# Turning the keys, queries and outputs of three batches on TensorE in place of DMA, under another written order

## The chip, the core and the metric

The kernel runs on one core of a Trainium2 chip. The core has a matrix engine (TensorE, "PE" in the profile, with its weight loads as "PEld"), a vector engine (VectorE, "DVE"), a scalar engine (ScalarE, "ACT"), GpSimd ("POOL") and the sync engine ("SP"), which here only issues transfers. Each works through a queue of its own, in order, and waits on semaphores for the others. The metric is the time of one execution on the device in microseconds (us); lower is better. Times of the kernel before: 255.43 us, the median of 3 runs (255.31 to 255.56).

## What is computed

Eight batches of eight heads, 576 positions, head size 64. First an attention with random features, then a gated long convolution on its output:

```python
def phi(x):                                   # 128 features for each position
    proj = einsum('bhsd,md->bhsm', x, omega)
    h = proj - sum(x * x, -1) / 2
    return exp(h - max(h)) / sqrt(m)
q_p, k_p = phi(q * scale), phi(k * scale)
kv  = einsum('bhsm,bhsd->bhmd', k_p, v);  z = sum(k_p, over s)
x   = (q_p @ kv) / (q_p @ z + 1e-6)           # batch, 576, 512

proj = x @ w_proj                             # 512 -> 3 * 512: x1, x2, x3
x2c  = irfft(rfft(x2, n=576) * rfft(filter, n=576), n=576)   # along the 576 positions
out  = (x1 * x2c * x3) @ w_out
```

## The kernel before

**Stages.** Positions are cut into four tiles of 128 and a rest of 64; the rests of two batches share a tile. `attention()` and then `hyena()` describe the work batch by batch. For a batch `b` the attention part does this. `turn_keys` brings the natural keys (positions on partitions) into the turned form `kt` (head dimension on partitions). `key_features` multiplies `kt` with the turned `omega` on TensorE, 64 rows to a matmul, and ScalarE takes the exponential into `ek`. VectorE finds the maxima of `ek` and scales the values into `vc` (`weigh_values`). `turn_queries` makes `qt`, and TensorE and ScalarE make `eqt`. "Sums" multiplies `ek` with `vc` into `kv`. "Turn out" multiplies `eqt` with `kv`, VectorE divides (`normalise`), and the result, with positions on partitions, is turned into `xt` (channels on partitions). `hyena()` handles two batches at a time: `fold`/`fold_rest` and `project2` for x2, `forward` (a Fourier transform as matmuls with tables, evicted into `sp`, whose two halves of partitions are swapped by two DMAs into a second `sp` tile, then multiplied with the filter's spectrum by VectorE in `spectrum`), `gates` (x1 and x3), "inverse", and "out" (the product with `w_out`, scaled by ScalarE, stored).

**Turning.** There are two ways. On TensorE, `transposes`, `turn_back` and `turn_runs` put eight 128x128 transposes (matmuls with the identity `ident`) into one bank of PSUM, named `h` (four such banks rotate among all users), and one copy brings the bank to SBUF: VectorE's for `kt`, ScalarE's for `qt` (from batch 2) and `xt`. By DMA, `cross` issues one transposing DMA on the SP queue for the whole tile. The table `CROSSED` (line 24) says from which batch on the DMA is taken. Before, it is batch 5 for keys, queries and outputs, so 9 transposing DMAs in all:

```python
crossed = {n: b >= first for n, first in CROSSED.items()}
def cross(dst, src):
    nc.sync.dma_start_transpose(out=dst, in_=src)
```

When outputs are crossed, `normalise` writes into `xb4`, one tile in the buffer `h1` that `max_to_c` uses too (one buffer); otherwise into four small buffers `xb`, which "inverse" shares for its `yc` and `yu`.

**Order.** Nothing runs in the order in which it is described. `Plan.record` (line 180) keeps every instruction as an operation with a number (matmuls into one bank in a row are one operation), and `Plan.issue` (line 232) issues them in the order of the list `ORDER` (line 26), which is written out by hand into the file and fixes the order of each engine's queue, the SP and POOL queues among them. Each number must stand behind those whose data it needs. As everything is issued from two lines, the profile's rows name L248 (a recorded operation) or L237 (below); one tells rows apart by the tiles that they write and read.

**Idle products.** `FILL` (line 91) names operations ahead of which `issue` puts a number of products of `ones` with itself (128x128 by 128 columns) into the bank that the operation is about to write. Their result is overwritten; they keep TensorE working. Before there are 139 of them at 8 places, on line 237, all in the first part of the kernel ("the ramp" below: the time until TensorE is steadily at work).

Of the kernel before, what the change touches and what calls it, by code (L numbers as in the profile page):

```python
# [13 lines left out]
BF16 = mybir.dt.bfloat16  # L14
# [6 lines left out]

P = 128

CROSSED = {"keys": 5, "queries": 5, "out": 5}

ORDER = """
0 38 43 35 28 30 29 32 44 36 31 33 40 37 39 34 1 8 5 41 42 49 50 51 4 45 140 7 22 56 55 3 11 53 21
10 54 52 2 48 139 68 6 46 23 24 62 25 142 63 64 66 26 75 15 47 57 65 82 83 58 60 59 103 61 101 81 76
77 79 584 84 67 89 69 17 102 78 588 80 605 70 71 90 73 72 157 85 138 587 104 586 74 111 113 115 117
158 137 105 91 151 159 210 106 143 107 108 92 93 94 152 161 112 95 96 97 114 12 9 589 160 165 162  # L30
109 116 163 13 118 590 110 99 164 153 209 166 591 595 20 155 154 156 167 119 120 127 128 130 131 129
145 87 183 184 86 227 124 16 132 125 126 221 121 122 98 185 123 228 630 628 631 645 647 641 18 629
599 598 168 100 186 187 135 136 133 230 646 19 134 173 233 234 222 169 175 146 232 620 144 632 170
174 612 176 594 606 171 593 172 597 633 592 229 231 614 621 178 180 224 613 637 636 643 622 181 642
147 149 662 212 148 226 215 182 663 615 623 211 177 179 204 205 634 596 206 624 14 635 247 664 191
192 194 195 193 248 667 207 638 616 196 640 668 208 626 235 688 218 281 236 188 189 245 690 190 197
293 246 639 618 198 199 223 225 287 200 201 294 689 691 237 608 202 259 203 256 625 238 694 258 692
261 288 239 319 712 644 693 609 240 627 666 713 761 320 697 249 250 695 585 283 217 150 677 610 655
665 213 763 679 219 214 284 678 681 669 611 216 704 290 696 657 292 656 658 659 710 296 298 684 251
252 253 363 762 764 141 705 241 295 297 708 711 600 601 243 709 603 260 289 291 262 602 364 661 357  # L40
757 730 731 670 671 254 255 257 358 263 264 648 728 699 276 672 303 242 304 305 277 660 273 274 680
278 275 301 729 759 302 649 346 617 676 675 366 698 673 360 306 619 362 706 707 299 265 726 758 368
220 282 244 266 703 702 727 300 701 267 700 307 760 685 365 359 361 367 674 769 724 771 268 650 351
654 269 682 345 270 356 725 753 321 313 315 271 770 385 386 322 755 323 308 754 272 387 388 772 756
314 309 311 316 733 718 279 280 369 317 318 716 732 683 719 734 370 310 312 735 872 736 371 714 372
285 715 686 717 340 373 341 604 335 336 342 765 687 383 767 384 343 720 381 332 721 344 857 337 858
423 653 374 333 334 867 723 722 607 382 776 778 327 742 743 324 338 286 339 325 326 777 744 745 746
396 865 780 328 375 866 329 651 779 747 652 398 934 766 936 330 349 417 88 376 331 869 868 870 871
389 768 859 352 740 741 861 790 792 426 378 737 860 390 738 881 739 429 481 348 347 748 749 942 944
428 943 885 791 945 886 431 873 793 794 773 787 775 876 751 874 788 875 395 930 932 397 931 887 789  # L50
888 933 796 425 774 427 483 392 394 950 889 935 795 882 377 379 878 782 750 890 952 430 391 449 879
781 783 893 937 432 450 894 393 907 752 399 472 479 400 908 883 433 451 797 877 784 862 880 804 884
806 801 350 803 409 818 820 863 815 903 798 452 802 410 434 435 411 901 436 473 484 864 453 904 902
412 897 353 355 354 424 898 816 817 486 799 785 413 800 819 905 895 488 414 786 822 821 896 437 938
404 415 405 438 823 906 909 910 940 401 416 838 839 824 951 805 402 406 380 478 825 891 892 403 494
495 808 482 444 446 807 439 441 953 407 919 912 911 809 913 422 447 920 496 408 448 923 917 921 497
498 922 499 810 918 924 490 500 954 467 1135 492 468 811 812 1050 501 983 985 899 840 956 469 900
955 957 939 440 442 443 445 947 941 915 946 958 491 948 1137 487 493 914 489 1051 813 916 814 826
949 827 828 925 960 829 969 971 1127 926 457 454 830 928 959 535 927 455 831 961 1129 456 475 418
477 847 848 849 470 853 460 929 471 854 856 1128 461 458 462 1130 474 421 480 966 970 972 973 835  # L60
463 967 968 836 419 1124 997 420 1011 1065 974 1059 464 999 1060 1013 459 465 1052 561 562 1123 1125
1053 984 855 485 1058 1063 541 538 1062 975 1126 543 540 841 980 1136 981 1061 837 987 976 466 986
512 542 982 977 1138 502 988 1064 832 1147 1066 1082 506 989 544 833 1149 1083 1054 1069 514 1055
1067 507 503 962 1080 1081 964 537 516 1078 1079 518 842 990 991 508 1074 1075 1068 1072 978 834 850
1096 1097 992 851 1076 539 963 509 1071 1025 1026 965 510 476 511 504 843 1070 1027 1077 1031 1032
1033 1100 1101 1008 513 517 1143 515 1012 519 1009 1145 520 545 546 993 536 852 1056 1014 521 1084
1016 547 1015 1057 1010 528 548 1017 1094 1073 529 979 530 994 522 523 1095 1085 995 996 998 1148
1000 505 524 531 1001 532 533 1090 1098 1099 1103 551 1091 1028 1029 1092 1102 525 553 549 1150 1002
526 527 1003 1004 1018 1139 1141 550 1086 1087 555 556 1022 1140 558 557 1110 1111 552 1005 1019
1007 563 564 565 1088 1021 1142 1046 1105 1104 554 559 534 1030 1093 1328 1089 560 1330 569 1258  # L70
1047 1048 1049 1106 570 1144 571 1108 1146 579 1020 1006 1114 1115 1320 1321 1243 580 1244 1176 1322
1023 1323 1178 1112 572 1162 1163 1164 1043 1107 573 1131 1113 1044 1024 1045 1133 1109 1329 574
1165 581 575 566 1166 1331 576 567 577 1132 1159 1160 1161 1177 1040 1134 582 1041 583 568 1252 578
1179 1167 1180 1168 1169 1259 1155 1116 1324 1173 1253 1251 1257 1256 1255 1117 1119 1042 1118 1326
1174 1175 1157 1156 1158 1267 1254 1262 1245 1275 1247 1325 1276 1332 1334 1246 1170 1260 1271 1327
1272 1273 1261 1268 1121 1266 1264 1181 1037 1265 1038 1269 1274 844 1281 845 1270 1293 1289 1282
1120 1182 1122 1171 1183 1172 1151 1294 1290 1153 1184 1204 1287 1206 1263 1185 1288 1291 1205 1190
1292 1295 1296 1333 1186 1208 1207 1248 1335 846 1340 1342 1192 1341 1152 1343 1187 1039 1191 1154
1193 1189 1194 1298 1249 1250 1188 1196 1195 1197 1198 1200 1034 1201 1283 1279 1035 1036 1202 1297
1299 1203 1284 1286 1285 1280 1199 1209 1300 1301 1210 1303 1277 1278 1309 1224 1310 1304 1305 1306  # L80
1225 1211 1212 1218 1219 1220 1307 1308 1312 1226 1370 1369 1371 1302 1214 1373 1372 1316 1366 1368
1367 1374 1375 1376 1213 1377 1344 1346 1345 1355 1318 27 1357 1221 1356 1347 1222 1239 1311 1236
1240 1237 1359 1313 1358 1314 1352 1317 1319 1349 1348 1350 1315 1223 1233 1238 1351 1353 1215 1360
1397 1234 1354 1242 1399 1241 1378 1383 1361 1379 1385 1216 1336 1338 1362 1363 1364 1394 1398 1395
1396 1337 1217 1235 1411 1400 1365 1412 1413 1417 1384 1401 1403 1402 1339 1380 1418 1419 1404 1382
1381 1414 1415 1387 1386 1389 1388 1390 1405 1391 1407 1416 1230 1231 1227 1228 1232 1408 1229 1409
1410 1393 1420 1421 1406 1392 1424 1436 1425 1430 1431 1437 1427 1428 1433 1434 1435 1423 1422 1426
1432 1438 1429
"""

FILL = {
    23: (40,), 75: (48,), 77: (13,), 89: (4,), 101: (6,), 103: (6,), 127: (12,), 135: (10,)
}

SIZE = {FP32: 4, UINT16: 2, BF16: 2, FP16: 2, mybir.dt.uint32: 4}
# [156 lines left out]
def kernel(  # L252
# [11 lines left out]
    nc = Plan(tc.nc, tc)  # L264
# [19 lines left out]
    const = ctx.enter_context(tc.tile_pool(name="const", bufs=1))  # L284
# [47 lines left out]
    def load_left(i, which):  # L332
# [3 lines left out]
        for j in range(2):  # L336
            nc.gpsimd.dma_start(
                out=t_[j * SL : (j + 1) * SL, :, :],
                in_=src[2 * i + j, :, SM:S, :].rearrange("h p d -> p h d"),
            )  # L340
        nat_tiles[which + "l", i] = t_

    nc.at("start", 0)
    nc.ones = nc.tile(const, [P, P], BF16, name="ones")
    nc.vector.memset(nc.ones[:], 1.0)
    om_f = nc.tile(hy, [P, D], FP32, name="osb", bufs=3)
    nc.sync.dma_start(out=om_f[:], in_=omega[:, :])
    ident = nc.tile(const, [P, P], BF16, name="ident")
    fi = nc.tile(const, [P, 5], FP32, name="fi")
    fp = nc.tile(const, [P, 1], FP32, name="fp")  # L350
    si = nc.tile(hy, [P, 512], FP32, name="osb", bufs=3)
# [43 lines left out]
    for j in range(2):  # L395
        nc.vector.tensor_scalar_mul(
            out=om2[j * D : (j + 1) * D, :], in0=omt[:D, :MF], scalar1=qk_scale
# [27 lines left out]
    gta = nc.tile(const, [P, CH], BF16, name="gta")  # L425
    gns = nc.tile(const, [P, 2, CH], BF16, name="gns")
    hps = nc.tile(const, [P, 5, DM], BF16, name="hps")
    hqs = nc.tile(const, [P, 5, DM], BF16, name="hqs")
    lo64, hi64 = slice(0, 64), slice(64, 128)

# [969 lines left out]
```

## Time and profile before

| | before |
|---|---|
| median of 3 runs | 255.43 us |
| the profiled execution's own time | 255.41 us |
| its span, first to last instruction | 253.6 us |
| around the span | 1.8 us |
| mean granted TensorE clock | 0.992 |
| PE busy | 236.9 us, 2370 matmuls in the records |
| VectorE busy | 225.7 us |
| ScalarE busy | 200.8 us |
| GpSimd busy | 59.4 us |
| bytes moved by DMA | 38.12 MB, mean 150 GB/s |
| transposing DMAs | 9, on the SP queue |

How to read it: a matmul's row gives the time from its start to the modelled end of its pipeline, so one of 128 columns shows 219 ns though the next may start sooner. The rate of a stream is read from the starts of rows that follow each other in the timeline. Busy time counts overlapping matmuls once. A few per cent of matmul records are missing.

### The profile page before, as it was taken

How to read it: one execution, taken by the hardware profiler on the slowest of the kernel's cores; microseconds unless marked ns; L12 is line 12 of the kernel's file. 1: busy time of each engine (PE TensorE's matmuls, PEld its weight loads, DVE VectorE, ACT ScalarE, POOL GpSimd, SP SyncE). 2: the span in 40 equal slices, each digit the busy share in tenths (PEclk: the TensorE clock that was granted, in tenths of full speed). 3: DMA queues.
4: the chain of work that ended last, by engine and by line, in shares of the span. 5: the costliest groups of instructions: out<-in, count | busy, mean ns of one | idle time of the engine just before them, and what ended most of it. 6: DMA issues, size and time to landing. Idle time of an engine off the chain costs nothing.

```text
span 253.6 us, 6119 instructions
## 1 busy us (share of the span) xinstructions
PE 236.9 (93%) x2370; PEld 142.6 (56%) x2404; DVE 225.7 (89%) x543; ACT 200.8 (79%) x322; POOL 59.4 (23%) x80
## 2 busy tenths in 40 slices
PE   6968988999999999998999998999999999998992
PEld 6946736645665655465645654564556545455641
DVE  6999999999998899997998998999898997986960
ACT  4799498999999998999779586987865664873772
POOL 8397531674106125700920000000000000000000
PEclk9988999999999999999999999999999999999999
DMA  6999999999949996996999491264622705254266
GB/s 78 186 189 191 206 181 201 221 176 197 209 71 172 184 193 118 165 154 138 189 172 155 144 193 49 85 165 108 124 85 76 173 3 161 67 166 127 83 248 210
DMA packets 87573, 38.12 MB, mean 150 GB/s; under 512 B 58427, under 2 KB 81912, under 8 KB 87544
## 3 DMA queue, kind: packets, MB, share of 16 engines
q0 software_dynamic: 59088, 16.85, 64.6%
q1 hardware_dynamic: 28312, 20.68, 33.4%
q8 instruction: 19, 0.31, 0.5%
q10 hardware_dynamic: 144, 0.20, 0.2%
q14 instruction: 10, 0.08, 0.1%
HBM read 33.72 MB, written 9.44 MB: 170 GB/s over the span
## 4 chain that ended last, share of the span: by engine, by line
PE 67%; ACT 11%; DVE 9%; DMA 8%; issue 3%; POOL 0%; SPq 0%; POOLq 0%; ACTq 0%; DVEq 0%
PE h L248 55%; PE a L248 12%; ACT ek L248 4%; DMA kt<-kn 4%; DVE sp L248 2%; DMA sp<-sp 2%; ACT eqt L248 2%; DMA xt<-h 2%; ACT osb L248 1%; ACT x L248 1%; DVE xb L248 1%; DVE yt L248 1%; DVE vc L248 1%; ACT L248 1%; DVE kt L248 0%
## 5 line engine op out<-in xcount | busy, mean ns | idle before, releaser
L248 PE MATMUL h<-xt,wproj 128*128 128x512 bf16 x242 | 62.7, 379 | 1.9 <-DMA xt<-h 0.6
L248 ACT CAST x<-h 128x512 bf16<-128x512 f32 x68 | 39.7, 603 | 16.6 <-PE h L248 9.6
L248 PEld LDWEIGHTS <-wproj 128*128 128x128 bf16 x384 | 30.6, 98 | 26.7 <-issue 2.9
L248 ACT ACTIVATE osb<-h 128x512 f32<-128x512 f32 (+4 forms) x53 | 30.2, 574 | 7.9 <-PE h L248 6.0
L248 ACT ACTIVATE eqt<-a 128x1024 bf16<-128x1024 f32 x32 | 32.7, 1049 | 1.1 <-PE a L248 1.1
L248 ACT ACTIVATE ek<-a 128x1024 bf16<-128x1024 f32 x32 | 32.6, 1048 | 0.4 <-PE a L248 0.2
L248 PE MATMUL h<-wproj,xf 128*128 128x512 bf16 x123 | 31.8, 379 | 0.4 <-issue 0.2
L248 PE MATMUL h<-wout,yt 128*128 128x512 bf16 (+2 forms) x128 | 31.2, 373 | 0.9 <-DVE x L248 0.7
L248 POOL DMA_DIRECT2D qn<-in_q_dram x26 | 23.4, 909 | 17.9 <-PE h L248 6.9
L248 DVE TENSOR_TENSOR x<-h,x 128x512 bf16<-128x512 f32 x32 | 21.6, 679 | 2.6 <-PE h L248 1.8
L248 ACT CAST sp<-h 128x512 bf16<-128x512 f32 x32 | 18.6, 614 | 4.3 <-PE h L248 4.2
L248 PEld LDWEIGHTS <-yt 128*128 128x128 bf16 x132 | 12.1, 98 | 13.7 <-issue 1.2
L248 PEld LDWEIGHTS <-xf 128*128 128x128 bf16 x128 | 11.6, 98 | 12.3 <-issue 0.9
L248 PEld LDWEIGHTS <-sp 128*128 128x128 bf16 x160 | 13.9, 98 | 5.5 <-DVE xf L248 0.2
L248 POOL DMA_DIRECT2D vn<-in_v_dram x8 | 7.2, 895 | 39.5 <-DVE vc L248 25.9
L248 DVE TENSOR_TENSOR xb<-a,rden 128x512 bf16<-128x512 f32 x24 | 16.0, 677 | 0.2
L248 PE MATMUL h<-x,fwb 128*128 128x512 bf16 x51 | 14.9, 379 | 0.1
L248 PE MATMUL a<-om,kt 64*128 64x128 bf16 x256 | 12.3, 223 | 2.0 <-DMA kt<-kn 0.7
L248 PEld LDWEIGHTS <-eqt 128*128 128x128 bf16 x256 | 11.3, 98 | 4.5 <-DVE xb L248 0.9
L248 PE MATMUL a<-kv,eqt 128*128 128x65 bf16 x256 | 12.8, 194 | 0.5 <-ACT ekl L248 0.2
L248 PEld LDWEIGHTS <-kt 64*128 64x128 bf16 x256 | 7.8, 96 | 9.4 <-issue 6.1
L248 PE MATMUL h<-gtab,sp 128*128 128x192 bf16 x64 | 12.8, 246 | 0.1
(156 smaller groups left out, 512.4 us busy)
## 6 DMA issues: line engine op xcount, KB each, us to landing
out_dram<-osb SPq DMA_DIRECT2D x24, 256.0 KB, 2.8
vn<-in_v_dram POOLq DMA_DIRECT2D x8, 512.0 KB, 8.4
sp<-sp SPq DMA_DIRECT2D x16, 256.0 KB, 3.5
kn<-in_k_dram POOLq DMA_DIRECT2D x7, 512.0 KB, 10.5
qn<-in_q_dram POOLq DMA_DIRECT2D x24, 128.0 KB, 7.9
wproj<-in_moe_w_proj_dram POOLq DMA_DIRECT2D x3, 512.0 KB, 11.6
qn<-in_q_dram POOLq DMA_DIRECT2D x2, 512.0 KB, 8.1
out_dram<-xf SPq DMA_DIRECT2D x4, 256.0 KB, 2.0
```

Of the source, the lines that this page charges most:

```text
L248: getattr(real, name)(*args, **kw)
```

## The change

`CROSSED` becomes 8 for all three, and there is no batch 8. So `cross` is never called, and the branches that batches 0 to 4 take are taken by 5 to 7 too. For each of these three batches, three transposing DMAs go, and six groups come: two for the keys (eight transposes and a VectorE copy each), two for the queries and two for the outputs (eight transposes and a ScalarE copy each). `normalise` then writes `xb` in place of `xb4`. The list has 1466 operations in place of 1439, is wholly rewritten, and numbers after batch 4 have moved. `FILL` holds 145 idle products at 11 places. `ones` has no tile of its own any more: it lies in the first 128 columns of `hps`, which is written with the filter's spectrum only later.

```diff
-CROSSED = {"keys": 5, "queries": 5, "out": 5}
+CROSSED = {"keys": 8, "queries": 8, "out": 8}
 ORDER = """
-0 38 43 35 28 30 29 32 44 36 31 33 40 37 39 34 1 8 5 41 42 49 50 51 4 45 140 7 22 56 55 3 11 53 21
...
-1432 1438 1429
+25 34 39 32 38 40 35 37 33 36 31 28 29 30 4 42 49 41 43 50 51 6 0 1 3 56 55 21 139 5 22 44 68 45 24
...
+1337 1395 1400 1399 1394 1242 1254 1261 1402 1390 1339 1401 1391 1403 1404 1405 1338 1341 1340 1342
+1375 1367 1255 1243 1244 1369 1438 1439 1377 1262 1256 1441 1442 1435 1436 1443 1440 1437 1376 1410
...
+1462 1459 1453 1465 1456
 """
 FILL = {
-    23: (40,), 75: (48,), 77: (13,), 89: (4,), 101: (6,), 103: (6,), 127: (12,), 135: (10,)
+    22: (25,), 69: (3,), 72: (7,), 75: (17,), 78: (61,), 89: (4,), 91: (8,), 101: (4,), 103:
+    (6,), 127: (6,), 157: (4,)
 }
...
     nc.at("start", 0)
-    nc.ones = nc.tile(const, [P, P], BF16, name="ones")
-    nc.vector.memset(nc.ones[:], 1.0)
...
     hps = nc.tile(const, [P, 5, DM], BF16, name="hps")
+    nc.ones = hps[:, 0, 0:P]
+    nc.vector.memset(nc.ones, 1.0)
```

## The prediction, on record before the result

> **What bounds the kernel now.** I read the page's busy times first, then busy time by stage, because a share over the whole span mixes stages.
>
> ```profile
> PE 236.9 (93%) x2370; PEld 142.6 (56%) x2404; DVE 225.7 (89%) x543; ACT 200.8 (79%) x322; POOL 59.4 (23%) x80
> ```
>
> ```profile
> core 0: us, PE busy (x) PEld busy (x) DVE busy (x) ACT busy (x) POOL busy (x), PEclk, DMA share, GB/s
> 0.00:60.00 60.00, 52.63 (x707) 36.57 (x711) 54.96 (x162) 49.95 (x65) 35.08 (x50) 0.97 1.54 181
> 60.00:160.00 100.00, 97.12 (x1002) 56.85 (x1015) 93.18 (x211) 88.96 (x142) 24.30 (x30) 1.00 1.16 153
> 160.00:222.00 62.00, 61.53 (x498) 34.44 (x505) 57.19 (x126) 43.92 (x82) 0.00 (x0) 1.00 0.43 107
> 222.00:245.00 23.00, 21.68 (x152) 12.91 (x153) 19.84 (x47) 14.79 (x32) 0.00 (x0) 1.00 0.45 147
> 245.00:253.60 8.60, 3.92 (x22) 1.80 (x21) 0.50 (x2) 3.16 (x6) 0.00 (x0) 0.98 0.64 221
> ```
>
> From 60 to 222 us TensorE is idle for 2.88 + 0.47 = 3.4 us of 162. Batches 5 to 7 are turned in this stretch (the transposing DMAs start between 77.3 and 194.3 us), so what the change adds to TensorE is added where it has no room. Only the ramp (7.4 us idle) and the end have room.
>
> The chain of waits names the DMA, and so would suggest that much is to be had:
>
> ```profile
> 105.83 0.36 PE a L248 x9
> 106.20 9.48 DMA kt<-kn
> 115.68 0.05 issue
> 115.72 0.40 PE a L248 x8
> ```
>
> But a step of the chain that runs through a DMA counts the whole flight, though TensorE does other work meanwhile. The timeline of TensorE shows what it lost:
>
> ```profile
> 114.38 0.59 PE L248 MATMUL h<-x,fwn 128*128 128x512 bf16 x2
> 115.72 0.40 PE L248 MATMUL a<-om,kt 64*128 64x128 bf16 x8 [0.75 <-DMA kt<-kn]
> ...
> 151.50 1.04 PE L248 MATMUL h<-wout,yt 128*128 128x512 bf16 x4
> 153.12 1.02 PE L248 MATMUL h<-xt,wproj 128*128 128x512 bf16 x4 [0.58 <-DMA xt<-h]
> ```
>
> **The change part by part.** *Transposes on TensorE.* Three batches, six groups each, eight transposes each: 144. Their nearest row is a group that already stands in a dense stretch:
>
> ```profile
> 146.29 0.59 PE L248 MATMUL h<-wproj,xf 128*128 128x512 bf16 x2
> 146.72 0.39 PE L248 MATMUL h<-ident,ql 128*128 128x128 bf16 x4
> 146.95 0.59 PE L248 MATMUL h<-xt,wproj 128*128 128x512 bf16 x2
> ```
>
> Two matmuls of 512 columns take 0.43 us from start to start, 0.215 each; the four transposes move the next start by 0.23 us, 56 to 57 ns each, with nothing lost going in or out. So 144 x 56 ns = 8.1 us, all of it on the path. Two rules of the Trainium skill speak for more. "TensorE: Matmul & The Clock Gate", section "Back-to-back issue gap", puts a stream of weight load and matmul at N=128 at about 81 ns each, which gives 11.7 us. Here each transpose has its own weight load and yet follows after 56 ns, so I take the row and keep 11.7 us for the range. The same page, "Part 4: PE-mode transpose", says that transposes don't count as activity for the clock gate. If turns let the clock fall to half, as it stands in one stretch of this trace (0.51 from 17.6 to 21.1 us), each would cost about 107 ns, 15.4 us together, and slow the matmuls around them. But 112 products with `ident` (transposes of batches 1 to 4 and of rests) lie between 60 and 160 us at a clock of 1.00. A group is 0.45 us long amid matmuls; I take no loss of clock there.
>
> *The transposing DMAs go.* TensorE gets back what the timeline shows: 115.72 - (114.38 + 2 x 0.215) = 0.9 us, and 153.12 - (151.50 + 4 x 0.215) = 0.8 us: -1.7 us. The bounds are 0 (the copy of the new group, or the next operand, is late at the same place) and -3.4 us (all idle time from 60 to 222 us). The SP queue also loses nine issues of 1.8 to 5.1 us; the stores and swaps behind them go earlier. From 60 to 160 us VectorE waits 0.7 us for a swap and TensorE never does, so I take 0 for it.
>
> *Copies.* Rows of the same operation:
>
> ```profile
> L248 ACT COPY qt<-h 128x1024 bf16<-128x1024 bf16 x6 | 6.2, 1038 | 0.0
> L248 DVE COPY kt<-h 128x1024 bf16<-128x1024 bf16 x10 | 6.8, 682 | 0.4 <-PE h L248 0.3
> ```
>
> Twelve ScalarE copies, eight of them for batches 5 and 6: 12 x 1.04 = 12.5 us. Six VectorE copies: 6 x 0.68 = 4.1 us. The division writes `xb` in place of `xb4` (677 against 688 ns): nothing. These lie beside TensorE's work: from 60 to 160 us ScalarE has 11 us to spare and VectorE 7 us, and the stretch itself grows by most of 8 us. I take 0. If that cover is gone, each of the 18 groups holds one of four `h` banks until its copy ends; TensorE losing 0.25 us at each would be +4.5 us. The wait that each copy adds stands in front of the evictions queued behind it, which is the way in which this would show.
>
> *The ramp.* Batches 5 to 7 are not in it; only the order and the idle products change. VectorE (14.1 of 15 us busy from 10 to 25 us, and again from 25 to 40) and ScalarE (14.2 of 15 from 10 to 25) set its pace. I added single durations in both written queues up to the point where TensorE has been given 16 and 32 us of its own work (56 ns for 128 columns, 216 for 512). VectorE has then been given 39.8 before and 38.0 after, and 59.6 before and 56.9 after; at 64 us, 92.5 and 93.5, and ScalarE 88.2 and 85.1. The two ramps are nearly alike, perhaps 1 us better. The first keys are loaded earlier in the POOL queue, but the first exponential still waits for the sines' residues on VectorE and for ScalarE's table loads. Six more idle products are 0.3 us where TensorE waits anyway: 0. A half-clock stretch of 3.4 us more or less is 1.7 us either way. I take -0.5 us, with -3 and +3 as bounds.
>
> *The end.* Before, TensorE has about 11.6 us of work queued between the last forward block of batch 7 and the first inverse block of batch 7, and still waits 0.55 + 0.66 us there. After, 8.5 us stand there (two inverse blocks of batch 6, seven blocks of four matmuls, two of 16). The data need: cast 0.6 and latency 0.2, second swap issued 0.5 later, 3.5 us (the median of the swaps) to 5.3 us (this one) to land, three products of 1.22 on VectorE: 8.5 to 10.3. So about 1 us idle, as before. Behind it VectorE has about 8.2 us to do before the last output blocks, plus 0.9 until its first input, while TensorE has 8.1: about 0.8 us more. Bounds -0.5 and +2.5.
>
> **Sum**, against the profiled execution's 255.4 us (span 253.6, 1.8 around it, within 0.02 of the median): 255.4 + 8.1 - 1.7 + 0 + 0 - 0.5 + 0.8 = 262.1 us.
>
> **The rivals.** *A, the forecast (0.60):* TensorE is full and takes the transposes at 56 ns: 259.5 to 265, likeliest 262.1.
>
> *B, the turns cost more than their columns (0.18):* copies and banks are the next thing late. Against it: VectorE and ScalarE have room on the average. For it: from 75 to 106 us ScalarE is busy 29.6 of 31 us. With 4.5 us lost at banks: 266.6, between 265 and 269.
>
> *C, the other order wins part of it back (0.12):* the ramp 3 us better and all idle time of the middle gone, 262.1 - 2.5 - 1.7 = 257.9, between 256 and 259.5.
>
> *D, it ends on the other side (0.10, of which 0.02 is no change):* the ramp is the lever. In the first 60 us TensorE is idle for 7.4 us and does 139 idle products (7.8 us): 15.2 us without use. If the new order halves that, 255.4 + 8.1 - 1.7 - 7.6 = 254.2. It decides from 6.4 us won in the ramp. Against it: VectorE is busy for 55 of those 60 us and is given the same work. That the change fails to do what it says can be left out: with 8 in the table no batch reaches `cross`.
>
> **How the numbers follow.** A difference under 0.2% (0.5 us) can't be told from no change here. Predicted 262.1, case A's. The range, 258.0 to 266.5, leaves out D and about half of B. Slower by over 0.2%: A, B and C, 0.90; within 0.2%: 0.02; faster: 0.08.
>
> **What would show it.** Right: no transposing DMA in the list of issues; 144 more products with `ident`, a group of eight moving the next start by 0.45 us; from 60 us on TensorE idle for no more than 3 us until the end; the time from 60 us to the last inverse blocks 6 to 8 us longer; ramp within 1 or 2 us. B shows as idle TensorE or weight loads ended by "ACT qt", "ACT xt" or "DVE kt". C and D show as TensorE reaching the same work of batches 1 and 2 earlier. I am wrong if the middle has room that busy time hides: matmuls count as busy until their modelled end, so small stalls are not seen, and fewer of them in another order would be a gain that no row here foretells.

## The result and the profile after

The kernel after takes 263.92 us (median of 4 runs, 263.01 to 264.29), against 255.38 us (255.31 to 255.56) for the kernel before, run beside it. The ratio is 1.0328 [1.0301, 1.0355]: slower, 1.8 us above the forecast of 262.1 and inside its range. The profiled execution took 264.05 us, with a span of 262.3 us, 8.7 more than before's.

The page's busy times of the kernel after:

```profile
PE 248.5 (95%) x2554; PEld 151.4 (58%) x2554; DVE 230.8 (88%) x549; ACT 212.9 (81%) x334; POOL 59.6 (23%) x80
```

By the pages TensorE is busy 11.6 us longer. Part of that is recording: before lacks the records of 34 of its 2404 matmuls (PE x2370, PEld x2404), after lacks none. Run 12 below has the order of before up to three moves near its end, and all its records. Its page:

```profile
PE 238.4 (94%) x2404; PEld 142.4 (56%) x2404; DVE 225.6 (89%) x543; ACT 200.8 (80%) x322; POOL 59.4 (24%) x80
```

Against this one, after is busy 10.1 us longer. ScalarE has 12.1 us more than before and VectorE 5.1, about the new copies (12.5 and 4.1 us in the forecast). The stages of after, cut as in the prediction:

```profile
core 0: us, PE busy (x) PEld busy (x) DVE busy (x) ACT busy (x) POOL busy (x), PEclk, DMA share, GB/s
0.00:60.00 60.00, 51.59 (x699) 36.78 (x700) 54.10 (x158) 48.54 (x64) 33.70 (x48) 0.97 1.52 173
60.00:160.00 100.00, 98.71 (x1077) 59.63 (x1076) 90.29 (x197) 88.03 (x134) 25.87 (x32) 1.00 0.99 129
160.00:222.00 62.00, 61.91 (x558) 35.60 (x557) 56.10 (x128) 51.97 (x90) 0.00 (x0) 1.00 0.21 64
222.00:245.00 23.00, 23.00 (x137) 12.02 (x135) 20.57 (x46) 15.43 (x31) 0.00 (x0) 1.00 0.44 133
```

From 60 to 222 us TensorE is idle for 1.29 + 0.09 = 1.4 us, and for none of the 23 us behind. The 3.4 us of before, which the prediction took as room, hold gaps where records are missing: run 12, with the same order there, is idle for 1.5 us. So TensorE was about as full before as it is after. The DMAs move less (share 1.16 to 0.99, then 0.43 to 0.21). The products with `ident`, by tile:

```profile
L250 PE MATMUL h<-ident,xb x144: 218/219/230, 31.8 to 211.7; 128*128 128x128 bf16 x144
L250 PE MATMUL h<-ident,kn x128: 217/219/230, 5.8 to 142.2; 128*128 128x128 bf16 x128
L250 PE MATMUL h<-ident,qn x128: 217/219/314, 12.5 to 181.3; 128*128 128x128 bf16 x128
```

Before, these counts are 96, 80 and 80: 48 more each, 144 together. The 219 ns of a row is no price. That is read from the starts of rows, here in TensorE's timeline of after:

```profile
209.09 1.03 PE L250 MATMUL h<-xt,wproj 128*128 128x512 bf16 x4
209.96 0.61 PE L250 MATMUL h<-ident,xb 128*128 128x128 bf16 x8
210.40 1.03 PE L250 MATMUL h<-wproj,xf 128*128 128x512 bf16 x4
211.27 0.61 PE L250 MATMUL h<-ident,xb 128*128 128x128 bf16 x8
211.71 1.03 PE L250 MATMUL h<-wproj,xf 128*128 128x512 bf16 x4
```

A group of eight moves the next start by 0.44 us, as forecast. All 18 new groups do so in this trace, by 0.44 to 0.46 us each and 8.04 us together, which is 56 ns for a transpose. From the matmul ahead of a group to its first transpose less than 0.01 us is lost, but for one group with 0.12. Between 60 and 245 us nothing waits for the new ScalarE copies; one wait of 0.4 us is for a new VectorE copy, of `kt` (waits of TensorE in after, total, times, longest):

```profile
PE h L250 <- DMA sp<-x: 0.7, 2, 0.4
PE h L250 <- DVE kt L250: 0.4, 1, 0.4
PE a L250 <- DVE vcl L250: 0.2, 1, 0.2
```

**Where the 8.7 us lie.** Busy time hides small stalls, so I matched each matmul record with its place in the written order and added columns at the rates of dense stretches: 56 ns for 128 columns, 82.5 for 192, 216 for 512, 30.5 for 65, and half of that for each of two matmuls on different 64 rows. This sum, without idle products, is TensorE's *own work*; what remains between two starts is *loss*. Own work is a count times a rate: its growth says how many columns were added, and only the starts say what they took. The ramp ends when 36 us of own work are done, the end begins when 27 us are left (differences are taken before rounding):

| us | before | after | difference | forecast |
|---|---|---|---|---|
| ramp: time until 36 us of own work are done | 61.8 | 63.4 | +1.6 | -0.5 |
| middle: own work | 150.0 | 158.0 | +8.0 | +8.1 |
| middle: loss | 8.4 | 9.4 | +0.9 | -1.7 (with the copies at 0) |
| end: time for the last 27 us of own work | 33.2 | 31.4 | -1.9 | +0.8 |
| span | 253.6 | 262.3 | +8.7 | |

The large term is right. The three small ones each miss by 2 to 3 us, two upwards and one downwards, and so the sum misses by only 2.

### The profile page after: what moved, and what is told of

The parts are those of the page before. It is cut to its first block, busy times and chain, and to the rows that moved or that the text cites. A ratio compares the mean times of both kernels' runs of the same rounds, so it can differ in the third digit from the quotient of the medians.

```text
span 262.3 us, 6466 instructions
## 1 busy us (share of the span) xinstructions
PE 248.5 (95%) x2554; PEld 151.4 (58%) x2554; DVE 230.8 (88%) x549; ACT 212.9 (81%) x334; POOL 59.6 (23%) x80
## 4 chain that ended last, share of the span: by engine, by line
PE 60%; DMA 18%; DVE 10%; ACT 4%; POOL 3%; issue 2%; SPq 2%; DVEq 0%; POOLq 0%; ACTq 0%
PE h L250 48%; PE a L250 10%; DMA vl<-in_v_dram 4%; DMA vn<-in_v_dram 3%; DMA sp<-sp 3%; DVE sp L250 3%; DMA hps<-osb 3%; DMA sp<-x 2%; DMA kn<-in_k_dram 2%; PE a L239 2%; SPq L250 2%; DMA xw<-xr 1%; ACT osb L250 1%; DVE vc L250 1%; DVE xb L250 1%
## 5 line engine op out<-in xcount | busy, mean ns | idle before, releaser
L250 PE MATMUL h<-xt,wproj 128*128 128x512 bf16 x256 | 64.3, 379 | 0.1
L250 ACT ACTIVATE osb<-h 128x512 f32<-128x512 f32 (+4 forms) x53 | 29.6, 570 | 6.8 <-PE h L250 5.2
L250 PE MATMUL h<-wout,yt 128*128 128x512 bf16 (+2 forms) x132 | 31.4, 373 | 0.0
L250 DVE TENSOR_TENSOR xb<-a,rden 128x512 bf16<-128x512 f32 x36 | 24.2, 682 | 0.7
L250 PEld LDWEIGHTS <-xf 128*128 128x128 bf16 x128 | 11.7, 98 | 13.1 <-issue 1.3
L250 ACT COPY xt<-h 128x1024 bf16<-128x1024 bf16 x16 | 16.3, 1025 | 0.4 <-PE h L250 0.2
L250 PE MATMUL h<-x,fwb 128*128 128x512 bf16 x56 | 15.5, 379 | 0.0
L250 PE MATMUL a<-qt,om 64*128 64x512 bf16 x64 | 11.8, 383 | 2.0 <-ACT eqt L250 0.9
L250 ACT COPY qt<-h 128x1024 bf16<-128x1024 bf16 x12 | 12.1, 1016 | 1.7 <-PE h L250 1.7
L250 PEld LDWEIGHTS <-eqt 128*128 128x128 bf16 x256 | 11.1, 99 | 3.6 <-issue 0.7
```

Of the source, the lines that this page charges most:

```text
L250: getattr(real, name)(*args, **kw)
```

## The experiments

The theory: TensorE is the full engine, a transposed tile costs its columns, and the DMAs' flight cost little. The rivals: a tile costs more (weight loads, clock, copies and banks), or not the turns but the new order makes the kernel slower. Ratios are to the kernel before.

**1. The 144 transposes twice** (the kernel after; the same eight written again into the same bank, the copies unchanged).

```diff
-        for g, src in enumerate(srcs):
-            nc.tensor.transpose(out=pb[:, g, :], in_=src, identity=ident[:])
+        for _ in range(2 if nc.where[0] in ("keys", "turn queries") and nc.where[1] >= 5 else 1):
+            for g, src in enumerate(srcs):
+                nc.tensor.transpose(out=pb[:, g, :], in_=src, identity=ident[:])
...
-        for g in reversed(range(n)):
-            nc.tensor.transpose(out=pb[:, g], in_=xbs[g // CB][:, g % CB], identity=ident[:])
+        for _ in range(2 if nc.where[0] == "turn out" and nc.where[1] >= 5 else 1):
+            for g in reversed(range(n)):
+                nc.tensor.transpose(out=pb[:, g], in_=xbs[g // CB][:, g % CB], identity=ident[:])
```

> The changed kernel, each of the 144 transposes of batches 5 to 7 issued twice into the same place, copies and order untouched. Theory (TensorE is full from 60 us on and a transpose costs its 128 columns, 56 ns): 144 x 0.0556 = 8.0 us more, 263.9 -> 271.9 us. Rival, transposes cost about 81 ns with their weight loads: +11.7, 275.6 us. Rival, transposes let the clock fall to half: +15 or more, over 279 us, and the granted clock under 0.97. Rival, the 8.5 us of the change come from the order and not from TensorE's columns: under +4, below 268 us.

Measured: 270.87 us (270.29 to 271.78), ratio 1.0599 [1.0568, 1.063], 7.0 us more than after. In the trace the 18 groups, now of 16 transposes each, move the next start by 16.1 us together in place of 8.0. The middle's loss falls from 9.4 to 8.8, and the ramp is 0.6 shorter. TensorE's timeline and windows of this run:

```profile
216.07 1.06 PE L250 MATMUL h<-ident,xb 128*128 128x128 bf16 x16
216.96 1.03 PE L250 MATMUL h<-wproj,xf 128*128 128x512 bf16 x4
```

```profile
60.00:160.00 100.00, 98.75 (x1113) 61.22 (x1112) 87.01 (x186) 84.94 (x130) 25.86 (x32) 1.00 0.97 121
160.00:230.00 70.00, 70.00 (x672) 42.48 (x670) 61.66 (x143) 55.98 (x97) 0.00 (x0) 1.00 0.24 70
```

With twice the turns the clock column still says 1.00. A transpose takes 56 ns here too; 81 ns (11.7 us more) and half clock (15.4 us more) are out.

**2. The 18 copies twice** (the kernel after; each copy of a new group issued again).

```diff
+        if nc.where[0] in ("keys", "turn queries") and nc.where[1] >= 5:
+            nc.ops[-1].calls.append(nc.ops[-1].calls[-1])
...
+        if nc.where[0] == "turn out" and nc.where[1] >= 5:
+            nc.ops[-1].calls.append(nc.ops[-1].calls[-1])
```

> The changed kernel, each of the 18 copies out of PSUM that belong to the turns of batches 5 to 7 issued twice in a row (12 on ScalarE of 1.03 us, 6 on VectorE of 0.68 us, so 12.4 and 4.1 us more work there). Theory (copies lie beside TensorE's work): +0 to +2, 264 to 266 us. Rival (the turns' cost is their copies and the banks they hold): the second copy costs what the first did, +4 or more, over 268 us.

Measured: 273.86 us (272.62 to 274.66), ratio 1.0708 [1.0671, 1.0746], 9.9 us more than after. My expectation failed. Own work is unchanged, the middle's loss grows from 9.4 to 18.2 us. The ramp is 1.8 us longer too, but no doubled copy lies in it; TensorE waits 1.8 us there for a load of queries. TensorE's waits in this run, 60 to 245 us:

```profile
PE h L250 <- ACT xt L250: 3.5, 4, 1.1
PE h L250 <- ACT qt L250: 1.4, 3, 0.6
PE h L250 <- DVE kt L250: 0.5, 2, 0.3
```

These are the rows that rival B named. 16.6 us of copies more cost 8.8 us in the middle: the room that busy time shows on ScalarE (12 of 100 us idle from 60 to 160 us) is not room for any copy at any place.

**3. The turns on TensorE in the order of before** (the kernel before; the nine DMAs replaced by 18 groups, each put some four TensorE blocks ahead of its first use; idle products, and `xb4` as the division's target, as before).

```diff
-CROSSED = {"keys": 5, "queries": 5, "out": 5}
+CROSSED = {"keys": 8, "queries": 8, "out": 8}
...
-                if crossed["out"]:
+                if b >= 5:
...
```

> The kernel before with its own order and idle products, but the nine transposing DMAs replaced by the 18 groups on TensorE and their copies, set some blocks ahead of their first use; the division still writes one tile. Theory (144 x 56 ns on a full TensorE; the order as such costs little): 255.4 + 8.0 - 0 to 1.7 for the DMA waits + 0 to 3 for places that were not sought out: 261.7 to 266 us. Rival (the new order is what costs): within 2 us of 255.4.

Measured: 267.72 us (266.91 to 268.94), ratio 1.0486 [1.0442, 1.053]: 12.3 us more than before, 1.7 above the range that I expected, and 3.8 more than the change itself. Own work +8.0; the middle's loss 14.2 in place of 8.4; ramp as before (61.8). Its waits of TensorE and of the weight loads:

```profile
PE h L247 <- ACT xt L247: 1.9, 3, 1.1
PE a L247 <- ACT sp L247: 1.1, 1, 1.1
PE h L247 <- ACT qt L247: 1.1, 2, 0.8
```

```profile
PEld L247 <- DVE kt L247: 2.1, 2, 1.6
```

So the new order doesn't make the kernel slow: with the same turns it wins 3.8 us. It places the copies so that TensorE waits 0.4 us for them in all; my placing did not. (The division's target and the idle products differ too; no run prices them apart.)

**4 to 6. One part at a time** (the kernel before; only the keys, only the queries, or only the outputs of batches 5 to 7 turned on TensorE, placed as in 3; the edit for the keys).

```diff
-CROSSED = {"keys": 5, "queries": 5, "out": 5}
+CROSSED = {"keys": 8, "queries": 5, "out": 5}
...
```

> Only the keys of batches 5 to 7 on TensorE (48 transposes, six VectorE copies), the rest as before. Theory: 255.4 + 2.7 - 0.9 for the keys' DMA wait + 0 to 2: 257 to 259.5 us. Rival (VectorE's copies hold TensorE up, as the waits for kt in the run with all three parts suggest): 260 or more.

> Only the queries of batches 5 to 7 on TensorE (48 transposes, six ScalarE copies). Theory: 255.4 + 2.7 + 0 to 2: 258 to 260 us.

> One part alone, in the order of the kernel before: only the outputs of batches 5 to 7 turned on TensorE (48 transposes, six ScalarE copies), keys and queries by DMA. Theory (56 ns each, -0.8 us for the wait for the output's DMA): 255.4 + 2.7 - 0.8 + 0 to 2 for banks held where no place was sought: 257 to 259.5 us. If the 12 us of the run with all three parts come from one part, it shows here or in the two next runs.

| | time | ratio | over before | own work | middle's loss |
|---|---|---|---|---|---|
| keys | 257.42 | 1.0079 [1.0056, 1.0103] | +2.0 | +2.7 | 10.0 |
| queries | 259.06 | 1.0138 [1.0101, 1.0174] | +3.7 | +2.7 | 11.1 |
| outputs | 260.80 | 1.0217 [1.0171, 1.0263] | +5.4 | +2.7 | 12.3 |

The 48 transposes count as 2.7 us of own work in each. Keys and queries came as expected; the outputs cost 1.3 us more than the top of what I expected. A group of outputs stands between the division and the projection, so it adds a wait on both sides, as TensorE's timeline of the outputs' run shows:

```profile
148.47 0.61 PE L246 MATMUL h<-ident,h 128*128 128x128 bf16 x8 [1.10 <-ACT xt L246]
...
176.26 0.62 PE L246 MATMUL h<-ident,h 128*128 128x128 bf16 x8 [0.90 <-DVE h L246]
```

The first waits for the copy that frees its bank, the second for the division. The three parts sum to 11.1 us; the three together, in run 3, cost 12.3.

**7. The DMAs back in the order of after** (the kernel after; keys and queries of batches 5 to 7 by DMA, each DMA as early in the order as the previous batch leaves its tile free).

```diff
-CROSSED = {"keys": 8, "queries": 8, "out": 8}
+CROSSED = {"keys": 5, "queries": 5, "out": 8}
...
```

> The changed kernel with its order, but keys and queries of batches 5 to 7 turned by DMA again (six DMAs, each set as early as the previous batch leaves the tile free); outputs stay on TensorE. Theory: 96 transposes fewer, -5.3 us, and waits for the DMAs where few blocks lie between (8 blocks of TensorE for the keys of batch 6 against a flight of 5 to 10 us, so some 3 us there): 258.5 to 262 us. Rival (TensorE's columns are not what the change costs): no gain, 264 us or more.

Measured: 275.28 us (273.65 to 275.6), ratio 1.0756 [1.0717, 1.0794], 11.4 us more than after and far above what I expected (258.5 to 262). Own work fell by 5.3 us, but losses rose by 16.5. TensorE's timeline shows the largest:

```profile
114.27 0.38 PE L246 MATMUL h<-x,fwa 128*128 128x512 bf16 x1
120.17 0.61 PE L246 MATMUL a<-om,kt 64*128 64x128 bf16 x8 [5.52 <-DMA kt<-kn]
```

A group is ready one copy after it is issued; this DMA of the whole tile was issued at 110.22 us and took 9.9 us to land, while TensorE had 4 us of work. It would have to stand well ahead in the order, and this order has no such place. The run shows the price of a DMA at a bad place, not that of a DMA.

**8. The 12 groups of keys and queries left out** (the kernel after; batches 5 to 7 use the turned keys and queries of batch 4).

```diff
-                kt = nc.tile(att, [P, H, 2, P], BF16, name="kt", bufs=1)
-                qt = nc.tile(att, [P, NT, NPAIR, P], BF16, name="qt", bufs=1)
+                if b < 5:
+                    kt = nc.tile(att, [P, H, 2, P], BF16, name="kt", bufs=1)
+                    qt = nc.tile(att, [P, NT, NPAIR, P], BF16, name="qt", bufs=1)
...
-                    if not crossed["keys"]:
+                    if b < 5:
...
-                    if not crossed["queries"]:
+                    if b < 5:
```

> The changed kernel without the twelve groups that turn keys and queries of batches 5 to 7: neither their 96 transposes nor their 12 copies; these batches use the turned keys and queries of batch 4 (so that part of the computation is left out), everything else in the same order. Theory (TensorE's columns are the whole price): -5.3 us, 258.6 us. If the copies cost as much as the doubled ones did (10 us for 18, 0.6 us each): a further -6 to -7, 252 us. Between the two: the copies' share in the change's own order.

Measured: 265.5 us (263.87 to 266.13), ratio 1.0396 [1.0353, 1.0439]: not faster than after, though 5.3 us of own work are taken away, and above all that I expected. The work that now comes earlier finds the filtered spectrum late (TensorE's timeline, with windows around the stall):

```profile
120.28 1.89 PE L246 MATMUL h<-xt,wproj 128*128 128x512 bf16 x7
124.98 0.26 PE L246 MATMUL h<-gta,sp 128*128 128x192 bf16 x1 [2.81 <-DVE sp L246]
```

```profile
118.00:121.80 3.80, 3.75 (x31) 1.96 (x30) 0.49 (x1) 3.62 (x6) 0.00 (x0) 1.00 0.73 177
121.80:125.20 3.40, 0.59 (x5) 0.22 (x4) 3.37 (x4) 0.68 (x2) 0.00 (x0) 1.00 0.40 154
125.20:128.80 3.60, 3.60 (x34) 2.95 (x32) 2.36 (x6) 2.07 (x5) 0.00 (x0) 0.53 0.02 5
```

Behind the stall the granted clock is 0.53 for 3.6 us, and 6.8 us of the ramp, which the edit leaves alone, are at half clock too. The run was to give the price of the first copies by difference, and gives none: a written order fits one set of durations.

**9 and 10. The ramps exchanged** (9: the kernel after, with before's order and idle products up to the 36 us of own work; 10: the kernel before with after's; the list is cut there and joined. The edit of 9, without the list).

```diff
-FILL = {
-    22: (25,), 69: (3,), 72: (7,), 75: (17,), 78: (61,), 89: (4,), 91: (8,), 101: (4,), 103:
-    (6,), 127: (6,), 157: (4,)
-}
+FILL = {22: (40,), 75: (48,), 77: (13,), 89: (4,), 101: (6,), 103: (6,), 127: (12,), 135: (10,)}
```

> The changed kernel, but everything up to where TensorE has been given 36 us of its own work stands in the order of the kernel before, with that kernel's idle products; the rest as in the changed one. By the two traces this point is reached at 61.8 us before and at 63.4 after. Theory (the new ramp costs 1.6 us): 262.3 us, if the joint costs nothing. If the ramp is no part of it: 263.9.

> The counterpart: the kernel before, with the changed kernel's order and idle products up to where TensorE has been given 36 us of its own work, and its own order and transposing DMAs behind that. Theory: 255.4 + 1.6 = 257.0 us, somewhat more if the joint costs. If the ramp is no part of it: 255.4.

Measured: 272.62 us (272.16 to 274.22), ratio 1.0696 [1.0654, 1.0738], and 261.91 us (261.85 to 262.86), ratio 1.0264 [1.0234, 1.0295]; I had expected 262.3 and 257.0. The totals decide nothing, since the joint costs more than the ramps differ: in 9 the losses from 60 to 100 us are 13.8 us, and in 10 TensorE stands still for 2.5 us at 146 us, waiting for a product of VectorE. The ramps themselves can be read. 36 us of own work are done at 61.5 us with before's ramp and at 63.1 with after's. Where `ones` lies is no part of this: run 9 has it in `hps` as after does, run 10 in a tile of its own as before does.

**11. More DMAs** (the kernel before; the queries of batches 3 and 4 by DMA too).

```diff
-CROSSED = {"keys": 5, "queries": 5, "out": 5}
+CROSSED = {"keys": 5, "queries": 3, "out": 5}
...
```

> The other direction: the kernel before, with the queries of batches 3 and 4 turned by DMA too (32 transposes and four ScalarE copies fewer, two transposing DMAs more, each set where the previous batch leaves the tile free, 15 and 19 blocks of TensorE ahead of the first use). Theory (each transpose is 56 ns of a full TensorE): -1.8 us, 253.6 us. Rival (a DMA in the stretch where 16 queues are busiest comes late): a wait of some us at the first query product of batch 3 or 4, 255 to 259 us.

Measured: 271.93 us (270.28 to 273.47), ratio 1.0657 [1.0603, 1.071], beyond my theory and its rival. The step the other way is no gain either. The SP queue, ScalarE and TensorE in this run:

```profile
63.21 5.04 SPq L246 DMA_TRANSPOSE qt<-qn  x1
68.31 0.57 SPq L246 DMA_DIRECT2D hqs<-osb  x1
...
70.85 1.23 SPq L246 DMA_DIRECT2D hps<-osb  x2
```

```profile
76.10 0.60 ACT L246 ACTIVATE osb<-h 128x512 bf16<-128x512 f32 x1 [9.21 <-DMA hqs<-osb]
```

```profile
77.66 0.60 PE L246 MATMUL a<-kv,eqt 128*128 128x65 bf16 x8 [8.70 <-ACT ek L246]
```

The transposing DMA holds SP's queue for 5.04 us. The filter's moves are queued behind it, they free `osb` late, ScalarE stands at the head of its queue for a free `osb`, and the exponentials behind it keep TensorE waiting 8.7 us. Two more waits are for transposing DMAs that land late, 4.2 us for `qt` and 1.9 for `kt`. So a turn by DMA isn't free: it costs its place in SP's queue. The order of before has places for nine, at which TensorE lost 1.7 us.

**12. The end alone** (the kernel before; the issue of the second swap, 1311, moved right behind the first, 1312; on VectorE a product of the inverse, 1358, ahead of the spectrum's first product, 1313, and a gate's product, 1319, ahead of its second, 1314).

```diff
-1225 1211 1212 1218 1219 1220 1307 1308 1312 1226 1370 1369 1371 1302 1214 1373 1372 1316 1366 1368
-1367 1374 1375 1376 1213 1377 1344 1346 1345 1355 1318 27 1357 1221 1356 1347 1222 1239 1311 1236
-1240 1237 1359 1313 1358 1314 1352 1317 1319 1349 1348 1350 1315 1223 1233 1238 1351 1353 1215 1360
...
+1224 1310 1304 1305 1306 1225 1211 1212 1218 1219 1220 1307 1308 1312 1311 1226 1370 1369 1371 1302
+1214 1373 1372 1316 1366 1368 1367 1374 1375 1376 1213 1377 1344 1346 1345 1355 1318 27 1357 1221
+1356 1347 1222 1239 1236 1240 1237 1359 1358 1313 1352 1317 1319 1314 1349 1348 1350 1315 1223 1233
...
```

> The kernel before with three moves near the end of its list and nothing else: the second swap DMA of batch 7's spectrum ahead of a store on the SP queue, and on VectorE two evictions that don't need the swap (one sum of the inverse of batch 6, one gate product of batch 6) ahead of the spectrum's products that wait for it. In the trace TensorE lost 0.55 and 0.66 us there because these evictions stood behind the wait. Theory: -0.5 to -1.2 us, 254.2 to 254.9 us. Rival (the wait moves to the first inverse block of batch 7): 255.4.

Measured: 254.06 us (22 runs, 252.82 to 256.35) against 255.38 (31 runs), ratio 0.995 [0.9929, 0.997]: 0.5% faster than before, small but clear of the noise. This version beats both kernels. VectorE before, then in this run:

```profile
230.39 1.22 DVE L248 TENSOR_TENSOR sp<-sp,hps 128x2048 bf16<-128x2048 bf16 x1 [1.94 <-DMA sp<-sp]
```

```profile
228.35 1.22 DVE L248 TENSOR_TENSOR sp<-sp,hps 128x2048 bf16<-128x2048 bf16 x1
```

VectorE no longer stands 1.94 us at the head of its queue, and TensorE's two stalls behind it (0.55 and 0.66 us before) are gone; its loss over the end falls from 1.6 to 0.1 us. The traces alone would not show that the order did it (see "The end" below); the 22 and 31 runs do.

## Why the prediction was right, and where its steps were wrong

**TensorE is the full engine, a transpose costs 56 ns (+8.1): right.** The 18 new groups take 8.04 us from start to start, and twice the transposes take 16.1 (run 1). Run 1 as a whole pays 7.0 us for them. The rule of the Trainium skill that I weighed against the row ("TensorE: Matmul & The Clock Gate", "Back-to-back issue gap", 81 ns) would have given 265.7. The total, 263.92, lies halfway between the two forecasts and tells nothing; the starts and run 1 decide for the row. That transposes don't keep the clock up (same page, "Part 4: PE-mode transpose") isn't seen in groups of up to 0.9 us amid matmuls: the clock is 1.00 over the middle of after and of run 1. No run here has a longer stretch of transposes.

**The DMAs' waits (-1.7): right in themselves.** The stalls at 115.72 and 153.12 us are gone. The chain's 9.48 us of flight were not to be had, as argued. The bound of -3.4 and the last 1.7 us of rival C were not to be had either: they count the missing records of before as idle time.

**The copies at 0: right for the waits that I named, but only in this order.** In the middle, after has no wait for `qt` or `xt` and one of 0.4 us for `kt`. Run 2 (+8.8 us of loss in the middle) and run 3 (5.8 us more loss in the middle) show how thin the cover is. In the forecast it was an average, "ScalarE has 11 us to spare and VectorE 7"; in the runs it is the place of each copy in its queue. Rival B was a real mechanism, which the change's own order avoids.

**The middle as a whole (-1.7 forecast, +0.9 measured): wrong by 2.6 us.** The step that failed is taking the gain of the two DMA waits as net: the rewritten order brought other losses. "Nothing lost going in or out" of a group came from one row, but it held for the 18 new groups. Losses over 0.3 us fell by only about half a us, the two DMA waits among those gone. New ones end at 64.91 and 65.72 us (waiting for a DMA of the filter), at 106.05 (for values from VectorE) and at 112.16 (for the `kt` copy). Losses of up to 0.3 us each rose by about 1.4 us, spread over many kinds of row and not at the new groups. Run 3, with all 18 groups in the old order, has about as much of them as after; runs 4 to 6, with 6 groups, have little more than before. What makes them is not settled.

**The ramp (-0.5 forecast, +1.6 measured): wrong, inside its bounds.** The step that failed is the sum of durations in the queues of VectorE and ScalarE: the after ramp has less of that work ahead of the same products, and is still later. Eight traces with before's ramp reach 36 us of own work at 61.5 to 62.0 us, six with after's at 62.8 to 65.2. Part of it may be the clock: five of these six traces have a stretch at half clock in the ramp, of 3.4 to 10.2 us; only two of the eight have one, of 3.4, and these two are no later than the other six. The chains of waits show what it does in after, where it lies over the sums of batch 0 (first after, then before):

```profile
23.98 2.18 PE a L250 x40
26.17 0.85 PE h L250 x8
```

```profile
24.23 1.42 PE a L248 x40
25.64 0.67 PE a L237 x12
```

The same 40 matmuls take 0.76 us longer. The window from 24 to 28 us of after shows a clock of 0.57 over them:

```profile
24.00:28.00 4.00, 4.00 (x68) 4.00 (x68) 2.93 (x5) 1.43 (x2) 2.12 (x4) 0.57 1.58 190
```

The trace of before has a half-clock stretch as long (3.4 us), but earlier, from 17.6 us. The clock is not the whole: about 1 us is there without any such stretch (62.8 us in run 1, whose ramp is after's), and of the four runs of after the one with a mean clock of 1.000 took 263.79 us, the others (0.991 to 0.993) 263.01 to 264.29. The cause of the rest stays open. The likeliest places are the losses from 20 to 40 us (9.2 against 6.3, idle products left out), but I have no run that removes one of them.

**The end (+0.8 forecast, -1.9 measured): wrong.** I took "about 1 us idle, as before" plus 0.8 of VectorE's work. After has no such gap there: its loss over the end is 0.4 us in place of 1.6, and 4.2 us lie behind the last matmul's start in place of 5.0. The step that failed is taking the gap in the one trace of before as a property of its order. The keys' run (4) has before's order there and neither stall. The second swap and VectorE's product behind it, before and then in that run:

```profile
224.66 0.65 SPq L248 DMA_DIRECT2D sp<-sp  x1
230.39 1.22 DVE L248 TENSOR_TENSOR sp<-sp,hps 128x2048 bf16<-128x2048 bf16 x1 [1.94 <-DMA sp<-sp]
```

```profile
228.80 0.67 SPq L246 DMA_DIRECT2D sp<-sp  x1
233.06 1.23 DVE L246 TENSOR_TENSOR sp<-sp,hps 128x2048 bf16<-128x2048 bf16 x1 [0.46 <-DMA sp<-sp]
```

From issue to product it is 5.7 us, then 4.3. Before's is the slowest of seven traces with this order there (3.8 to 5.7 us); the other six need 31.2 to 32.5 us for the end, four of them no more than 31.7, near after's 31.4. So most of the -1.9 is not shown to be the new order's. Run 12 shows besides that the order can take the wait off VectorE's path, which I had not considered.

So 262.1 was near 263.92 because +2.1 (ramp) and +2.6 (middle) stand against -2.7 (end), which is luck. The large term carried the sign; the small terms were within their bounds but for the end.

## What to carry to other kernels

Where the timeline shows an engine without gaps, moving work onto it costs that work's full issue time, and a DMA's flight on the chain of waits is no measure of what its removal gives back: take the gaps of the full engine, after a check that its records are complete. Room on a side engine is a question of places, not of averages: double the side work once and see. In a kernel with a written order, an edit without a new order mostly prices the order, so read each part from its own waits and not from the total.

## What the runs showed of the hardware

A stall of TensorE can cost twice. In run 8 a stall of 2.8 us is followed by 3.4 us at half clock. In run 11 the clock falls during the stall, which begins at 68.96 us (windows):

```profile
68.50:71.80 3.30, 0.46 (x3) 0.10 (x1) 0.85 (x2) 0.00 (x0) 0.00 (x0) 0.99 1.37 180
71.80:82.00 10.20, 4.12 (x30) 2.05 (x30) 3.08 (x9) 3.50 (x5) 0.00 (x0) 0.50 0.66 91
```

The clock falls 2.8 us into the stall, and 10.2 us are at half clock. The mean clock of this run is 0.965, of run 7 0.963, and of after 0.993. The length of the stall does not decide it alone: run 10's stall of 2.5 us at 146 us is followed by none of it (1.00 from 149 to 155 us), a stall of 1.9 us in run 11, up to 132.55 us, by 3.4 us from 133.2. In run 8, 5.3 us of work taken off the full engine so gained nothing.
